# RWKV attention and a leaky-ReLU MLP: w loaded into all partitions and as columns, stage 1 in float32 by hardware queues, dummy matmuls until the first turning

## The chip, the cores and the metric

The kernel runs on one core of a Trainium2 chip. Five engines with instruction streams of their own work side by side and meet at semaphores: TensorE (PE, matmuls), VectorE (DVE), ScalarE (ACT), GpSimd (POOL) and SyncE (SP, here only transfers). The metric is the device time of one execution in microseconds, the median of several runs. A profiled execution shows when each instruction ran; its span goes from the first to the last instruction.

## The reference

Linear attention with a decaying state, over batch 4, 8 heads, 768 positions and head width 48, and behind it an MLP with a leaky ReLU:

```python
state = zeros((B, H, D, D))
for t in range(S):
    kt, vt, rt = k[:, :, t], v[:, :, t], r[:, :, t]
    cur = einsum('bhd,bhe->bhde', u[None] * kt, vt)
    y[:, :, t] = einsum('bhd,bhde->bhe', rt, state + cur)
    state = w[None, :, :, None] * state + einsum('bhd,bhe->bhde', kt, vt)
x = y.transpose(0, 2, 1, 3).reshape(3072, 384)
h = x @ w_in                      # 384 x 2048
out = maximum(0.01 * h, h) @ w_out  # 2048 x 384
```

All inputs and the output are float32; w and u are one vector of 384 numbers each (8 heads times 48).

## The kernel before

**Tiling.** The 4 x 768 positions are cut into 24 stages of 128 (`L`), six to a batch. Inside a stage, the positions lie on the 128 partitions. Powers of w are put into two tables, `qtab` = w^(t-64) and `ktab` = w^(63-t), one row for each position t of the stage, 384 columns. They are the exponentials of t times ln w, so that r * qtab and k * ktab carry the decay between two positions.

**One stage n** goes through named steps:

- P (`prep`): DVE multiplies r by qtab and k by ktab into `qk`, in bf16. r comes first, then k.
- T (`turn`): PE turns the products with the identity (two halves, four matmuls each) into PSUM, and ACT copies both halves into `tp`. From stage 8 on a transfer does this instead.
- A (`a_mm`): eight matmuls of turned k and turned r give the 128 x 128 scores of each head. M (`a_mask`): DVE multiplies them by a triangular mask into `at`.
- X (`diag`): DVE multiplies turned r by turned k into `prod`. K (`kv_mm`): PE multiplies `prod` by the column w*u (`wu`), which gives the share of the current position, and k by v for the state. Q (`prep2`) puts the first into `vs` on DVE. S (`state`): DVE multiplies the new state by the decay table `wl` = w^128.
- Y (`y_part`): PE adds everything up, ACT copies it into `xT`.
- G, J: first matrix product of the MLP (`g1`, `g1_pair`) with the leaky ReLU on ACT; H and `g2_seven`: the second product.

**Order.** Every engine executes its instructions in the order in which `add` was called; semaphore waits come from what is read and written. Up to stage 9 the order is written out by hand in `ORDER`, a list of these letters with the stage's number. Then a loop over pairs of stages goes on. PSUM banks are handed out in rotation by `next_bank`, eight in all.

**Opening.** w and u arrive as one row on one partition each (SP's and ACT's queue). r and k of stage 0 come as float32, r on SP's queue and k on ACT's. All other tiles of r, k and v are cast to bf16 by POOL's queue, one after another, together with the MLP's weights, in the order of `LOADS`. In that list `id` and `tri` stand for the identity and the triangular mask, which POOL makes between its transfers; `wi` and `wo` are the four parts of w_in and of w_out. PE runs `EARLY` = 2 dummy matmuls of 128 x 512 (L255), then spreads the row of w over 128 partitions with two matmuls against a row of ones (L295). ACT takes the logarithm from PSUM in two halves (L298) and makes the tables (L299, L301). The step C (`decay_columns`, L449) turns w and w*u from rows into columns with sixteen matmuls of one column; ACT takes the logarithm of one (`wcol`, L465) and DVE copies the other (`wu`, L467). The step W (`decay_table`, L471) makes `wl` on ACT (L474). U (`u_table`) spreads u over the partitions later on; the cast of u's row to bf16 (L303) stands in the opening.

The lines that the text speaks of are L327 and L329 (P), L379 and L386 (matmuls and copies of T), L399 (A), L417 (M), L334 (X), L429 to L438 (K), L342 (Q), L483 (S), L518 (Y), L546 and L563 (G and J).

Of the kernel before, what the change touches and what calls it, by code (L numbers as in the profile page):

```python
# [17 lines left out]
E = 64  # L18
# [5 lines left out]
FIRST, EARLY = 6, 2  # L24
LOADS = """r1 k1 r2 id k2 wi0 v1 r3 tri k3 v2 wi1 k4 r4 v3 wi2 k5 r5 r6 k6 v4 v5 k7 wi3 r7 v6 v7 wo3 wo2 wo1 wo0"""
ORDER = """
P0 C W P1 T0 A0 X0 M0 T1 P2 K0 A1 T2 Q0 X1 Y0 A2 S0 M1 K1 X2 G0.0 Q1 P3 S1 Y1 T3 K2 M2 G1.0 X3 A3 U J0.2 S2 Q2 M3 Y2 K3 P4 T4 Q3
J0.3 S3 Y3 J0.4 J0.5 J1.0 P5 A4 J1.1 P6 X4 M4 T5 X5 J1.2 K4 Q4 A5 S4 T6 J1.3 K5 J1.4 Y4 M5 L8 Q5 Y5 P7 J1.5 A6 J0.6 J2.0 J2.1 T7
M6 X6 X7 K6 J2.2 J2.3 A7 S6 J2.4 J2.5 L9 Q6 J0.7 J1.6 J2.6 M7 L10 J2.7 L11 J1.7 K7 S7 P8 Q7 Q8 P9 H0 Q9 K8 H1 P10 L12 K9 H2 S8 S9
Y6 Y7 A8 A9 P11 M8 H3 M9 L13  # L30
# [90 lines left out]
def bass_rwkv5_eagle__then__act_leaky_relu_kernel(  # L121
# [13 lines left out]
    def SB(name, shape, dt=BF16):  # L135
        return ctx.enter_context(nc.sbuf_tensor(name, shape, dt))
# [11 lines left out]
    w_row = SB("w_row", [1, HD], FP32)  # L148
    u_row = SB("u_row", [1, HD], FP32)
    one_row = SB("one_row", [1, 128], FP32)  # L150
# [4 lines left out]
    k0_f = SB("k0_f", [128, HD], FP32)  # L155
    r0_f = SB("r0_f", [128, HD], FP32)
# [6 lines left out]
    wu_row = SB("wu_row", [1, HD])  # L163
# [27 lines left out]
    taken = [0]  # L191
# [9 lines left out]
    def load_first(which):  # L201
        src = {"k": k, "r": r}[which][0].rearrange("h t d -> t h d")[0:L, :, :]
        dst = {"k": k0_f, "r": r0_f}[which]
        eng = {"k": "act", "r": "sp"}[which]
        queue = {"k": A, "r": SP}[which]
        add(eng, lambda: queue.dma_start(dst[:, :].rearrange("p (h d) -> p h d", d=D), src),
            W=[(which, 0)], dma=f"{which}0")
# [38 lines left out]
    add("dve", lambda: V.memset(one_row[:, :], 1.0), W=["one_row"])  # L246
# [12 lines left out]

    half_w = [(next_bank(), slice(NH * i, NH * i + NH)) for i in range(2)]  # L260
# [9 lines left out]
    for name in LOADS.split():  # L270
# [15 lines left out]
    add("dve", lambda: V.memset(v_sb[:, :, :].rearrange("p n (h e) -> p (n h) e", e=E)[:, :, D:E], 0.0), W=["v0"])  # L286
    add("dve", lambda: V.tensor_tensor(wu_row[:, :], w_row[:, :], u_row[:, :], ALU.mult),
        R=["w_row", "u_row"], W=["wu_row"])
# [3 lines left out]
    add("dve", lambda: V.memset(wu[:, :, :], 0.0), W=["wu"])  # L292
    fill(EARLY)
    for (ps_w, key_w), cols in half_w:
        add("pe", lambda ps_w=ps_w, cols=cols: PE.matmul(ps_w[:, 0:NH], one_row[:, :], w_row[:, cols], start=True, stop=True),  # L295
            R=["one_row", "w_row"], W=[key_w, "bc"])
    for i, ((ps_w, key_w), cols) in enumerate(half_w):
        add("act", lambda ps_w=ps_w, cols=cols: A.activation(lnw[:, cols], ps_w[:, 0:NH], AF.Ln), R=[key_w], W=[("lnw", i)])  # L298
        add("act", lambda cols=cols: A.activation(qtab[:, cols], lnw[:, cols], AF.Exp, scale=qexp[:, 0:1]),  # L299
            R=[("lnw", i), "qexp"], W=[("qtab", i)])  # L300
    add("act", lambda: A.activation(ktab[:, :], lnw[:, :], AF.Exp, scale=kexp[:, 0:1]),  # L301
        R=[("lnw", 0), ("lnw", 1), "kexp"], W=["ktab"])
    add("act", lambda: A.activation(u_row16[:, :], u_row[:, :], AF.Copy), R=["u_row"], W=["u_row16"])  # L303
# [5 lines left out]
    def k_of(n):  # L309
        return k_sb[:, n % NRK, :] if n else k0_f[:, :]  # L310

    def r_of(n):
        return r_sb[:, n % NRK, :] if n else r0_f[:, :]

    def prep(n):
        iq = n % NQK
        if n >= TURNED:
            both = rk_sb[:, n % NRK, :, :].rearrange("p w (h d) -> p (w h) d", d=D)
            by = tab[:, :, :].rearrange("p w (h d) -> p (w h) d", d=D)
            add("dve", lambda: V.tensor_tensor(qk[iq][:, :, 0:D], both, by, ALU.mult),  # L320
                R=[("r", n % NRK), ("k", n % NRK), ("qtab", 0), ("qtab", 1), "ktab", ("qk0", iq)], W=[("qp", iq), ("kp", iq)])
# [5 lines left out]
        add("dve", lambda: V.tensor_tensor(qk[iq][:, 0:H, 0:D], hd(r_of(n)), hd(qtab[:, :]), ALU.mult),  # L327
            R=[("r", n % NRK), ("qtab", 0), ("qtab", 1), ("qk0", iq)], W=[("qp", iq)])
        add("dve", lambda: V.tensor_tensor(qk[iq][:, H:2 * H, 0:D], hd(k_of(n)), hd(ktab[:, :]), ALU.mult),  # L329
            R=[("k", n % NRK), "ktab", ("qk0", iq)], W=[("kp", iq)])  # L330
# [40 lines left out]
    def turn(n):  # L371
        it, iq = n % NTP, n % NQK
        for half in ((0, 1) if n == 0 else (1, 0)):
# [75 lines left out]
    def decay_columns():  # L449
        ps_c, key_c = next_bank()  # L450

        def emit():
            for hh in range(2):
                for p in range(NP):
                    c0 = (2 * p + hh) * D
                    rows = slice(64 * hh, 64 * hh + D)
                    PE.matmul(ps_c[rows, p:p + 1], w_row[:, c0:c0 + D], one_row[:, 0:1], start=True, stop=True)
                    last = PE.matmul(ps_c[rows, NP + p:NP + p + 1], wu_row[:, c0:c0 + D], one_row16[:, 0:1],
                                     start=True, stop=True)
            return last  # L460

        add("pe", emit, R=["one_row", "one_row16", "w_row", "wu_row"], W=[key_c, "wcols"])
# [269 lines left out]

    def u_table():
# [5 lines left out]
    steps = {"U": u_table, "P": prep, "Q": prep2, "T": turn, "A": a_mm, "M": a_mask, "K": kv_mm, "S": state, "Y": y_part, "X": diag, "C": decay_columns, "W": decay_table, "F": fill,  # L739
# [118 lines left out]
```

## Time and profile before

| | us |
|---|---|
| median of 3 runs | 168.59 (167.9 to 169.27) |
| the profiled execution | 168.52 |
| its span | 166.8 |
| PE busy | 160.0 |
| DVE busy | 120.3 |
| ACT busy | 116.6 |
| POOL busy | 81.8 |

The profiled execution took 168.52 us as timed, of which the span of the trace is 166.8; the rest lies outside the instructions. Busy time is the sum over an engine's instructions; matmuls overlap, so that a busy PE isn't one at its peak. "L255 PE MATMUL a<-b x2" reads: line 255, engine, operation, result and operands, number. A bracket gives the idle time in front of an instruction and what ended it. "Landing" of a transfer is the time at which its semaphore says that all of it is there.

### The profile page before, as it was taken

The numbers are of one execution on the slowest core, as the hardware profiler recorded it, in microseconds if no ns is written. First come the engines' busy times: TensorE is split into PE (matmuls) and PEld (weight loads), VectorE is DVE, ScalarE is ACT, GpSimd is POOL, SyncE is SP. The second block draws the span as 40 slices with busy tenths as digits, with TensorE's granted clock in tenths as the row PEclk, the third lists the DMA queues.
The fourth block names the chain that finished last, engine by engine and source line by source line (L and its number), as shares of the span: only waits on it lengthen the run. The fifth ranks groups of instructions, "written<-read, shape, count | busy, mean of one in ns | idle before, by whom it ended". The sixth has DMA issues, their size and how long they took to land.

```text
span 166.8 us, 5326 instructions
## 1 busy us (share of the span) xinstructions
PE 160.0 (96%) x2264; PEld 132.2 (79%) x2264; DVE 120.3 (72%) x231; ACT 116.6 (70%) x265; POOL 81.8 (49%) x97
## 2 busy tenths in 40 slices
PE   6699999999999999999999999999999999999994
PEld 3578677788666875875876889889899898898993
DVE  7697866653898969999359997986998467046253
ACT  4944877798313771879989889989999845828530
POOL 7999999991179989795660750930000000000000
DMA  5999999999989999999995994995706202002022
GB/s 95 112 146 171 171 149 173 201 192 141 142 201 150 129 92 92 135 162 107 176 178 55 207 119 76 188 114 94 132 4 139 81 4 94 4 4 94 0 98 94
DMA packets 99259, 19.68 MB, mean 118 GB/s; under 512 B 92322, under 2 KB 99236, under 8 KB 99236
## 3 DMA queue, kind: packets, MB, share of 16 engines
q0 software_dynamic: 76512, 10.03, 94.4%
q1 hardware_dynamic: 21682, 9.11, 25.7%
q8 instruction: 18, 0.29, 0.7%
q10 hardware_dynamic: 1042, 0.20, 0.6%
q14 instruction: 5, 0.04, 0.1%
HBM read 20.45 MB, written 4.72 MB: 151 GB/s over the span
## 4 chain that ended last, share of the span: by engine, by line
PE 90%; ACT 5%; DVE 2%; issue 1%; ACTq 0%
PE ps_all L563 36%; PE ps_all L644 20%; PE ps_all L580 16%; PE ps_all L518 7%; PE ps_all L399 5%; ACT tp L386 2%; PE ps_all L433 2%; PE ps_all L379 2%; DVE at L417 1%; PE ps_all L546 1%; PE ps_all L255 1%; PE ps_all L295 1%; ACT tab L299 1%; ACT wl L474 0%; ACT gT L569 0%
## 5 line engine op out<-in xcount | busy, mean ns | idle before, releaser
L563 PE MATMUL ps_all<-xT,w_in_sb 128*128 128x256 bf16 x564 | 64.8, 273 | 0.0
L563 PEld LDWEIGHTS ps_all<-xT,w_in_sb 128*128 128x128 bf16 x564 | 54.3, 98 | 7.2 <-issue 0.2
L569 ACT ACTIVATE gT<-ps_all 128x512 bf16<-128x512 f32 x94 | 55.1, 598 | 6.8 <-PE ps_all L563 2.9
L218 POOL DMA_DIRECT2D rk_sb<-in_k_dram x23 | 21.3, 928 | 16.6 <-PE ps_all L563 16.6
L580 PE MATMUL ps_all<-w_out_sb,gT 128*128 128x384 bf16 x160 | 27.2, 326 | 0.0
L409 DVE CAST_PREDICATED at<-mask,ps_all 128x1024 bf16<-128x1024 uint16 x16 | 18.8, 1219 | 9.2 <-PE ps_all L399 9.2
L367 ACT ACTIVATE at<-ident,s_tok 128x128 bf16<-128x128 bf16 x80 | 24.9, 393 | 0.0
L580 PEld LDWEIGHTS ps_all<-w_out_sb,gT 128*128 128x128 bf16 x160 | 15.3, 98 | 9.7
L218 POOL DMA_DIRECT2D v_sb<-in_v_dram x24 | 22.3, 934 | 0.4 <-issue 0.4
L218 POOL DMA_DIRECT2D rk_sb<-in_r_dram x23 | 21.1, 919 | 0.0
L361 POOL TENSOR_TENSOR at<-ident,s_tok 128x512 bf16<-128x512 bf16 x12 | 13.4, 1140 | 10.4 <-DVE s_tok L351 10.4
L675 DVE TENSOR_TENSOR out_sb<-ps_all,snap 128x192 f32<-128x192 f32 x22 | 7.8, 356 | 14.5 <-PE ps_all L644 13.8
L644 PE MATMUL ps_all<-tw,gs 128*128 128x192 bf16 x168 | 16.0, 246 | 0.0
L586 ACT ACTIVATE out_sb<-ps_all 128x384 f32<-128x384 f32 x10 | 4.9, 488 | 14.5 <-PE ps_all L580 14.4
L644 PEld LDWEIGHTS ps_all<-tw,gs 128*128 128x128 bf16 x168 | 14.0, 98 | 0.0
L533 ACT ACTIVATE xT<-ps_all 128x384 bf16<-128x384 f32 x24 | 11.0, 492 | 4.0 <-PE ps_all L518 3.7
L518 PE MATMUL ps_all<-at,v_sb 128*32 128x128 bf16 x384 | 11.9, 224 | 0.0
L417 DVE TENSOR_TENSOR at<-ps_all,mask 128x512 bf16<-128x512 f32 x16 | 10.3, 683 | 2.2 <-PE ps_all L399 1.9
L618 DVE TENSOR_TENSOR gs<-gT 128x1024 bf16<-128x1024 bf16 x14 | 9.6, 685 | 2.9 <-ACT gT L569 2.9
L644 PE MATMUL ps_all<-w_out_sb,gT 128*128 128x192 bf16 x112 | 11.6, 246 | 0.0
L386 ACT ACTIVATE tp<-ps_all 128x512 bf16<-128x512 f32 x16 | 8.7, 596 | 3.8 <-PE ps_all L379 3.7
L518 PEld LDWEIGHTS ps_all<-at,v_sb 128*32 128x32 bf16 x384 | 9.1, 98 | 2.3 <-issue 1.1
(80 smaller groups left out, 217.5 us busy)
## 6 DMA issues: line engine op xcount, KB each, us to landing
out_dram<-out_sb SPq DMA_DIRECT2D x22, 192.0 KB, 2.4
v_sb<-in_v_dram POOLq DMA_DIRECT2D x24, 96.0 KB, 5.9
rk_sb<-in_r_dram POOLq DMA_DIRECT2D x23, 96.0 KB, 6.0
rk_sb<-in_k_dram POOLq DMA_DIRECT2D x23, 96.0 KB, 5.7
w_in_sb<-in_moe_w_in_dram POOLq DMA_DIRECT2D x4, 384.0 KB, 7.0
w_out_sb<-in_moe_w_out_dram POOLq DMA_DIRECT2D x4, 384.0 KB, 9.7
out_dram<-out_sb SPq DMA_DIRECT2D x4, 96.0 KB, 1.6
tp<-qk SPq DMA_TRANSPOSE x16, 3.4
```

What stands on the lines that cost most here:

```text
L218: add("pool", lambda: G.dma_start(dst, src), R=pace, W=[key], dma=f"{which}{n}")
L361: add("pool", lambda hh=hh, s_of=s_of: G.tensor_tensor(at[ia][:, hh, :, :], ident[:, :].unsqueeze(1).to_broadcast([128, NP, 128]), s_of.un ...
L367: add("act", lambda h=h: A.activation(at[ia][:, h % 2, h // 2, :], ident[:, :], AF.Copy, scale=s_tok[n % 2][:, h:h + 1]), R=["ident", ("s" ...
L386: add("act", lambda dst=dst, ps_t=ps_t: A.activation(dst, ps_t[:, :], AF.Copy), R=[key], W=[("tp", it, half)])
L409: add("dve", lambda: V.copy_predicated(at[n % NAT][:, :, :, :].rearrange("p two m i -> p (two m) i"), mask[:, :].bitcast(mybir.dt.uint16). ...
L417: add("dve", lambda hh=hh, part=part: V.tensor_tensor(at[n % NAT][:, hh, :, :], part, mask[:, :].unsqueeze(1).to_broadcast([128, NP, 128]) ...
L518: last = PE.matmul(ps_y[32 * q:32 * q + 32, 128 * s:128 * s + 128], a, m, start=first_mm, stop=last_mm)
L533: add("act", lambda: A.activation(xT[m % NX][:, :, 128 * half:128 * half + 128], ps_y[:, 0:HD].rearrange("p (s t) -> p s t", t=128), AF.Copy),
L563: last = PE.matmul(ps_g[:, 256 * f:256 * f + 256], w_in_sb[:, s, 128 * fb:128 * fb + 128], xT[ix][:, s, :], start=s == 0, stop=s == NSL - 1)
L569: add("act", lambda: A.activation(gT[ig][:, 2 * j:2 * j + 2, :].rearrange("p f t -> p (f t)"), ps_g[:, :], AF.Prelu, alpha=0.01), R=[key], ...
L580: last = PE.matmul(ps_o[:, 0:HD], gT[ig][:, s, 128 * half:128 * half + 128], w_out_sb[:, s, :], start=s == 0, stop=s == NFB - 1)
L644: done = PE.matmul(ps_o[:, 0:NH], lhs[:, s, :], rhs[:, s, :], start=first and s == 0, stop=s == HF - 1, skip_group_check=not (first and last))
```

## The change

w is loaded by one transfer into all 128 partitions (`w_all`), so the broadcast matmuls and one pair of activations go. w and u are also loaded as columns, two transfers for each (`load_columns`, pieces of 4 bytes), and step C becomes step B, which takes Ln of the one and multiplies the two on DVE. r and k of stage 1 come like those of stage 0, as float32 on SP's and ACT's queue, ahead of the columns; they leave POOL's list. The identity and the mask stand further ahead in that list. u's row comes last on SP's queue, and its cast is a step of its own (V). `EARLY` goes from 2 to 8 dummies, and two single dummies (F1) are put into the order. T1 is cut into its two halves, the half with r in front of A0. `taken` starts at 3, so that later banks are the same as before. DVE's memset of the gaps in v moves behind the other memsets.

```diff
-FIRST, EARLY = 6, 2
-LOADS = """r1 k1 r2 id k2 wi0 v1 r3 tri k3 v2 wi1 k4 r4 v3 wi2 ...
+FIRST, EARLY = 6, 8
+LOADS = """r2 id k2 tri v1 wi0 r3 k3 v2 wi1 k4 r4 v3 wi2 ...
 ORDER = """
-P0 C W P1 T0 A0 X0 M0 T1 P2 K0 A1 T2 Q0 X1 Y0 A2 S0 M1 K1 X2 G0.0 Q1 P3 S1 Y1 T3 K2 M2 G1.0 X3 ...
+P0 T0 P1 B T1.0 F1 A0 T1.1 X0 M0 K0 W P2 F1 A1 V T2 Q0 X1 Y0 S0 M1 K1 A2 X2 G0.0 Q1 P3 S1 Y1 T3 K2 M2 G1.0 X3 ...
...
-    def load_first(which):
-        src = {"k": k, "r": r}[which][0].rearrange("h t d -> t h d")[0:L, :, :]
-        dst = {"k": k0_f, "r": r0_f}[which]
+    def load_first(n, which):
+        src = {"k": k, "r": r}[which][0].rearrange("h t d -> t h d")[n * L:n * L + L, :, :]
+        dst = {"k": k_f, "r": r_f}[which][n]
...
+    def load_columns(h, dst, name):
+        for hh in range(2):
+            add("sp", lambda hh=hh: SP.dma_start(dst[64 * hh:64 * hh + D, :], dram(h, D * hh, [[1, D], [2 * D, NP]]),
+                                                     allow_slow_non_contiguous=True),
+                W=[f"{name}{hh}"], dma=f"{name}{hh}")
...
-    add("sp", lambda: SP.dma_start(w_row[:, :], row(w)), W=["w_row"], dma="w")
-    add("act", lambda: A.dma_start(u_row[:, :], row(u)), W=["u_row"], dma="u")
-    load_first("r")
-    load_first("k")
+    add("sp", lambda: SP.dma_start(w_all[:, :], dram(w, 0, [[0, 128], [1, HD]])), W=["w_all"], dma="w")
+    load_first(0, "r")
+    load_first(0, "k")
+    load_first(1, "r")
+    load_first(1, "k")
+    load_columns(w, w_col, "wc")
+    load_columns(u, u_col, "uc")
+    add("sp", lambda: SP.dma_start(u_row[:, :], row(u)), W=["u_row"], dma="u")
...
-    for i, ((ps_w, key_w), cols) in enumerate(half_w):
-        add("act", lambda ps_w=ps_w, cols=cols: A.activation(lnw[:, cols], ps_w[:, 0:NH], AF.Ln), R=[key_w], W=[("lnw", i)])
-        add("act", lambda cols=cols: A.activation(qtab[:, cols], lnw[:, cols], AF.Exp, scale=qexp[:, 0:1]),
-            R=[("lnw", i), "qexp"], W=[("qtab", i)])
+    add("act", lambda: A.activation(lnw[:, :], w_all[:, :], AF.Ln), R=["w_all"], W=["lnw"])
+    add("act", lambda: A.activation(qtab[:, :], lnw[:, :], AF.Exp, scale=qexp[:, 0:1]), R=["lnw", "qexp"], W=["qtab"])
...
-    def turn(n):
+    def turn(n, *halves):
-        for half in ((0, 1) if n == 0 else (1, 0)):
+        for half in halves or ((0, 1) if n == 0 else (1, 0)):
...
     def decay_columns():
-        ps_c, key_c = next_bank()
...
         for hh in range(2):
             rows = slice(64 * hh, 64 * hh + D)
-            add("act", lambda rows=rows, hh=hh: A.activation(wcol[rows, :], ps_c[rows, 0:NP], AF.Ln),
-                R=[key_c], W=[f"wcol{hh}"])
-            add("dve", lambda rows=rows, hh=hh: V.tensor_copy(
-                wu[rows, :, hh:hh + 1].rearrange("p m o -> p (m o)"), ps_c[rows, NP:2 * NP]),
-                R=[key_c, f"wcol{hh}", "wu"], W=[f"wu{hh}"])
+            add("act", lambda rows=rows: A.activation(wcol[rows, :], w_col[rows, :], AF.Ln),
+                R=[f"wc{hh}"], W=[f"wcol{hh}"])
+            add("dve", lambda rows=rows, hh=hh: V.tensor_tensor(
+                wu[rows, :, hh:hh + 1].rearrange("p m o -> p (m o)"), w_col[rows, :], u_col[rows, :], ALU.mult),
+                R=[f"wc{hh}", f"uc{hh}", "wu"], W=[f"wu{hh}"])
```

The step B stands behind P1 on DVE, and its Ln stands on ACT between the copies of T0 and those of T1; W follows the copies of T1, behind them V. A2 has moved behind K1. From there on ORDER is unchanged.

More of the change, by code (lines that the diff above doesn't have):

```diff
@@ L154, in bass_rwkv5_eagle__then__act_leaky_relu_kernel @@
     u_tab = SB("u_tab", [128, HD])
-    k0_f = SB("k0_f", [128, HD], FP32)
-    r0_f = SB("r0_f", [128, HD], FP32)
+    k_f = [SB(f"k{i}_f", [128, HD], FP32) for i in range(2)]
+    r_f = [SB(f"r{i}_f", [128, HD], FP32) for i in range(2)]
     tab = SB("tab", [128, 2, HD])
@@ L258, in fill @@
         add("pe", emit, R=["ones"], W=[("ps", i), f"fill{n}"])
-    half_w = [(next_bank(), slice(NH * i, NH * i + NH)) for i in range(2)]
     def identity():
@@ L292, in bass_rwkv5_eagle__then__act_leaky_relu_kernel @@
     add("dve", lambda: V.memset(wu[:, :, :], 0.0), W=["wu"])
+    add("dve", lambda: V.memset(v_sb[:, :, :].rearrange("p n (h e) -> p (n h) e", e=E)[:, :, D:E], 0.0), W=["v0"])
     fill(EARLY)
[L294 to L303 removed]
+    add("act", lambda: A.activation(lnw[:, :], w_all[:, :], AF.Ln), R=["w_all"], W=["lnw"])
+    add("act", lambda: A.activation(qtab[:, :], lnw[:, :], AF.Exp, scale=qexp[:, 0:1]), R=["lnw", "qexp"], W=["qtab"])
+    add("act", lambda: A.activation(ktab[:, :], lnw[:, :], AF.Exp, scale=kexp[:, 0:1]), R=["lnw", "kexp"], W=["ktab"])
     at_bank, kv_bank = {}, {}
@@ L309, in k_of @@
     def k_of(n):
-        return k_sb[:, n % NRK, :] if n else k0_f[:, :]
+        return k_sb[:, n % NRK, :] if n > 1 else k_f[n][:, :]
     def r_of(n):
-        return r_sb[:, n % NRK, :] if n else r0_f[:, :]
+        return r_sb[:, n % NRK, :] if n > 1 else r_f[n][:, :]
     def prep(n):
```

42 lines of the change are left out of this document (15 added, 27 removed).

## The prediction
> **What bounds the kernel now.** I read the page first, then the busy time in windows, the chain of waits, and the opening instruction by instruction.
>
> ```profile
> span 166.8 us, 5326 instructions
> PE 160.0 (96%) x2264; PEld 132.2 (79%) x2264; DVE 120.3 (72%) x231; ACT 116.6 (70%) x265; POOL 81.8 (49%) x97
> PE   6699999999999999999999999999999999999994
> ```
> TensorE (PE) is busy for 160.0 of 166.8 us, and its idle time lies almost wholly in the first three slices. The change touches nothing behind the first fifteen microseconds, so only that stage can give or take time. In windows:
>
> ```profile
> 1.40:5.00 3.60, 3.35 (x22) 2.08 (x22) 3.22 (x14) 2.50 (x5) 3.59 (x4) 1.00 1.17 142
> 5.00:8.00 3.00, 1.75 (x23) 1.36 (x21) 2.16 (x6) 2.90 (x9) 3.00 (x6) 1.00 2.18 113
> 8.00:10.60 2.60, 2.01 (x24) 1.60 (x24) 1.92 (x5) 1.36 (x3) 2.60 (x4) 1.00 1.07 128
> 10.60:14.30 3.70, 3.62 (x61) 2.70 (x62) 3.13 (x8) 1.61 (x4) 3.70 (x6) 1.00 2.31 160
> ```
> The first pair of numbers is the window and its length, the next is PE's busy time. Between 5.0 and 10.6 PE idles 1.25 + 0.59 us; afterwards it is full. ACT is the full one between 5 and 8 (2.90 of 3.00). The chain of waits goes through it:
>
> ```profile
> 4.79 0.46 ACT tab L299
> ...
> 6.83 0.36 ACT wl L474
> ...
> 7.21 1.09 ACT tp L386 x2
> ...
> 8.35 0.61 PE ps_all L399 x8
> ...
> 15.73 0.70 PE ps_all L518 x40
> ...
> 17.95 0.43 DVE prod L334
> 18.38 0.47 DVE st L483
> 18.85 0.46 DVE vs L342
> 19.31 1.20 DVE at L417 x2
> 20.51 0.26 DVE qk L327
> 20.77 0.28 DVE qk L329
> ...
> 23.05 2.07 PE ps_all L563 x18
> ```
> Tables of w (tab), then the decay columns and table (wcol, wl), hold ACT until 7.19; only then come the copies of the first turning (tp), and A0 starts on PE at 8.35. Around 18 to 21 us the chain lies on VectorE (DVE). From about 23 us it is solid PE work, so what the stage ahead gains or loses is passed to the end nearly whole.
>
> A second thing binds this stage: the same PE instructions are slow first and fast later.
>
> ```profile
> 1.65 1.04 PE L255 MATMUL ps_all<-ones 128*128 128x512 bf16 x2 [1.65 <-DVE ones L247]
> 10.68 0.61 PE L399 MATMUL ps_all<-tp 48*128 48x128 bf16 x8 [0.32 <-ACT tp L386]
> 11.22 1.04 PE L379 MATMUL ps_all<-ident,qk 128*128 128x128 bf16 x8
> L546 PE MATMUL ps_all<-xT,w_in_sb x12: 227/314/314, 14.3 to 15.5; 128*128 128x128 bf16 x12
> 16.33 0.62 PE L379 MATMUL ps_all<-ident,qk 128*128 128x128 bf16 x8
> ```
> Eight turnings take 1.04 us at 11.22 and 0.62 at 16.33, and within the twelve matmuls of L546 the duration falls from 314 ns to 227 for the last, at 15.5. The windows' column of granted clock stays at 1.00, so it isn't the throttle that the profile lists. PE had run without a break since 10.68, that is 4.8 us, when it became fast.
>
> **The change part by part.** The rows for the opening:
>
> ```profile
> 1.19 0.43 SPq L206 DMA_DIRECT2D r_f<-in_r_dram  x1
> 1.34 0.41 ACTq L206 DMA_DIRECT2D k_f<-in_k_dram  x1
> 1.78 1.28 ACT L242 ACT_TABLE_LOAD   x1 [1.78 <-PEq L843]
> 2.45 0.89 POOL L218 DMA_DIRECT2D rk_sb<-in_r_dram  x1
> 2.61 1.14 PEld L295 LDWEIGHTS ps_all<-w_row,one_row 1*128 1x128 f32 x4 [0.84 <-DMA w_row<-in_w_dram]
> 5.15 0.60 ACT L301 ACTIVATE tab<-lnw,kexp 128x384 bf16<-128x384 f32 x1
> 5.34 0.74 DVE L327 TENSOR_TENSOR qk<-r_f,tab 128x384 bf16<-128x384 f32 x1 [0.45 <-DVE wu L292]
> 6.00 0.55 DVE L329 TENSOR_TENSOR qk<-k_f,tab 128x384 bf16<-128x384 f32 x1
> 6.84 0.36 DVE L327 TENSOR_TENSOR qk<-rk_sb,tab 128x384 bf16<-128x384 bf16 x1
> 7.46 0.36 DVE L329 TENSOR_TENSOR qk<-rk_sb,tab 128x384 bf16<-128x384 bf16 x1 [0.26 <-DMA rk_sb<-in_k_dram]
> 9.11 1.29 DVE L417 TENSOR_TENSOR at<-ps_all,mask 128x512 bf16<-128x512 f32 x2 [0.35 <-POOL mask L267]
> ```
> Transfers, from the list of issues (median to landing in us) and from the packets in the window 3.0 to 4.0:
>
> ```profile
> r_f<-in_r_dram SPq DMA_DIRECT2D x1, 192.0 KB, 3.5
> k_f<-in_k_dram ACTq DMA_DIRECT2D x1, 192.0 KB, 4.0
> q10 hardware_dynamic: 821, 0.16, 77.7%
> q1 hardware_dynamic: 532, 0.10, 49.3%
> ```
> and in the window 4.0 to 4.5, q10 (ACT's queue, k0) alone:
>
> ```profile
> q10 hardware_dynamic: 192, 0.03, 48.2%
> ```
> So r0 landed at 1.19 + 3.5 = 4.7 and k0 at 1.34 + 4.0 = 5.3. Two hardware queues together moved 821 + 532 = 1353 packets in that microsecond: 0.76 us for a float32 tile of 1024 packets of 192 bytes. k0's last 192 packets fell in the next half microsecond, so some 0.8 to 1.0 us passed between its last packet and its landing.
>
> Tables. Gone are the broadcast by two matmuls (L295), one Ln, one Exp and the detour through PSUM. New is w in 128 partitions: 192 KB, priced between nothing and a whole tile's 0.76 us more than the single row, which was there at 2.6. I take 0.6, being few long pieces, plus the sharing with k0: about 3.4. The table load ends at 3.06, so it doesn't bind. Then three activations at ktab's 0.60 at most, qtab ready at 4.6 and ktab at 5.2. r0 now stands behind w on SP's queue and shares with k0 and, soon, k1: w (0.6), k0 and r0 (0.76 each) from about 2.0 make 4.1 to 4.3 for the last packet, and 0.8 to landing: 5.05. P0 starts there instead of 5.34: **0.3 us won**. DVE's memsets ahead of P0, in another order now, were through at 4.89 (P0's q had waited 0.45 at 5.34) and there is one memset and one multiplication less: they stay covered by r0, and would bind only if it came before then.
>
> Turning. P0's q ends at 5.8, its k at 6.3; four turnings each, then two copies of half of 1.09 each, now directly behind ktab: done at 7.55 instead of 8.30, **0.75 us won** in all so far. The eight dummies run 7 steps of 0.42 (1.04 less one duration of about 0.62) and one 0.62, 3.56 us from about 1.45: they end at 5.0, before P0's q, and cost nothing unless P0 came sooner. The sixteen small matmuls of the old columns leave a window in which PE idled anyway: nothing.
>
> Stage 1. r1 and k1 leave POOL's queue (two issues of 0.89 us, so everything behind them is issued 1.8 us sooner) and stand behind r0 and k0 on SP and ACT. From 4.0 three queues share the engines: r1, k1 and POOL's v0 are 3 x 0.76 = 2.3 us, with r0's rest until 6.5; landing at 7.3 to 7.4. In the old run P1's q started at 6.84 without waiting for its tile, and its k waited until 7.46. So r1 is **0.5 us later**, not sooner, and P1 in float32 takes 0.55 to 0.74 for each half, not 0.36. The page "DMA: Bandwidth & Descriptors" of the Trainium skill (section "Issuing engines are not separate DMA queues") speaks against this part too: every queue ends on the same 16 engines, and more of them save issue time alone. The packet rows agree, and the sum is made from them.
>
> The new order puts T1.0 before A0. PE is in order, so A0 waits for P1's q: 7.4 + 0.6 = 8.0, four turnings 0.5, one dummy 0.45, A0 at 8.9 instead of 8.35 and ready at 9.5. M0 starts there instead of at 9.11; its mask, which held M0 for 0.35 us before, now stands further ahead in POOL's queue and is ready. Behind it T1.1 and K0 come no later than before. **0.4 us lost** at M0, which takes the whole gain of the head. This 0.4 goes along DVE through P2, Q0, X1 and S0 to M1, which starts at 12.5.
>
> Columns. Four transfers of 192 pieces of 4 bytes replace 16 matmuls, a copy and ACT's Ln on PSUM. They stand behind r1 on SP's queue. If a piece costs what a packet does, 4 x 192 / 1353 = 0.57 us, doubled by sharing with POOL: last packet near 7.6, landing 8.5. DVE reaches wu at about 8.5, behind it X0, which must be done before M0 at 9.5. Price: nothing; the other end is a rival below. The decay table, two activations of 0.36, stands behind T1's copies now, which end at about 10.5, and S0 asks for it at about 12: covered by 0.8 us. A2 stands behind K1 and so waits for S0, done by 12.5, but M2 asks for it only at 15.6: nothing.
>
> The clock. With T1.0, dummy, A0, T1.1, K0, dummy, A1 and T2 PE now has work without a gap from 8.0. If it takes the same 4.8 us as before, it is fast at 12.8, and no later than 2.6 us ahead of the old 15.4. DVE, back to back from M1 at 12.5, has by the chain's rows M1 1.20, X2 0.43, Q1 0.46 (to 14.6), P3 0.54, S1 0.47 and M2 1.20 and is free at 16.8. Y1 follows Q1 with 0.70 at the fast rate, T3's first half needs about 0.35 and its copies 1.09: 16.8 too. X3 can start at 16.9 to 17.0 instead of 17.95. From there to T4 the steps are the old ones: **0.95 us won**. The transfers allow it: POOL's loads come nearly a microsecond sooner, having lost 1.8 us of issue, while the engines carry 1.2 us of new traffic but start on it sooner. Sum: 168.52 (the profiled execution; 1.7 us of it lies outside the span) less 0.95 is 167.57. The median of the runs is 168.59, the same within 0.1: **167.6**.
>
> **The rivals.**
> A, the eight dummies open the clock already at about 5 us. They are 3.56 us of unbroken work, against 4.8 in the old run, which is only an upper bound of what is needed. The page "TensorE: Matmul & The Clock Gate" of the Trainium skill (Part 1) says that the array starts at half clock and that some 3.4 us of sustained work opens it, by a window that runs freely and so ends anywhere in a kernel. Then A0's 0.61 and the turnings' 1.04 shrink like the 0.62 above, M0 starts at 8.85, and DVE is the bound, back to back: M1 at 11.85, 4.3 us from there to the end of M2, X3 at 16.2 and, 0.43 + 0.47 + 0.46 later, M3 at 17.55 instead of 19.31: 1.75 us, 166.8. For it: the length. Against: PE idles again from 5.0 to 5.8 and from 6.9 to 8.0.
>
> B, PE is fast no sooner, because its work before 11 us is of matmuls on 48 rows and short ones. Then the 0.2 to 0.4 us lost at M0 stays: 168.8. For it: the stretch from 8.35 to 10.36 was full as well and changed nothing.
>
> C, slower: the columns come late. If each of the four tiny transfers costs by itself what k0 spent between its last packet and its landing, about 1.0 us, they end at 7.4 + 4.0 = 11.4. DVE waits there in order, with X0, M0, P2 and everything behind queued, and K0 waits on PE; M0 starts at 12.2 instead of 9.5, 2.7 us on top of the sum: 170.3. From 9.6 on it takes back the whole gain, 1:1. For it: pieces of 4 bytes occur nowhere in the trace. Against: the packets' number is small.
>
> That the change doesn't do what it says, for instance that w in all partitions lands later than 4.5, would be covered by the wait for r1, which ends at 7.4 anyway.
>
> **How the numbers follow.** My forecast 38%, A 22%, B 22%, C 18%. About 1% (1.7 us, below 166.9 or above 170.3) is what can be told from no change. Faster: the lower two thirds of A, whose centre lies at the limit and which gains more if A0 comes sooner, and a little of the forecast's lower side, 0.20. Slower: half of C and the tail of B if r1 is later still, 0.12. The rest, 0.68, lies within. The range runs from 0.7 below A, for a sooner M0, to just short of C's centre: 166.1 to 170.0. It leaves out the upper half of C, B's tail and A's edge. The forecast's own range is 167.0 to 168.3.
>
> **What would show it.** P0's q near 5.05, tp's copies directly behind ktab and done near 7.5; r_f's second transfer landing at 7.3, T1.0 on PE at 8.0 with a wait for DVE's qk; M0 at 9.5; the durations of L379's and L546's successors falling from 314 to about 220 ns between 11 and 13 us (at 5 in A, at 15 in B); no wait for a column's transfer before wu (over 0.8 us in C); X3 near 17.0. I am wrong if r1 lands before 6.8, if wu waits, or if solid PE work starts more than a microsecond away from where the sum puts it.

## The result and the profile after

The changed kernel took 173.18 us (median of 4 runs, 172.66 to 174.24), the kernel before 168.69 on the same chip: a ratio of 1.0277, 95% interval 1.0211 to 1.0343. It is slower by 2.8%; 167.6 had been forecast, with a range up to 170.0. Where a ratio stands beside a median below, the ratio leaves out executions more than 1.5% above the fastest one of their kernel.

The profiled execution took 173.44 us, its span 171.7. The page's span, PE's busy tenths and the granted clock in 40 slices of 4.3 us:

```profile
span 171.7 us, 5285 instructions
...
PE   6179999969999999999999999999999999999993
...
PEclk9955899999999999999999999999999999999999
```

PE is all but empty in the second slice, has a new hole in the ninth, and this page has a row of granted clock, which the page of before lacks. The opening instruction by instruction (start, duration, engine, line, operation; in the bracket the idle time ahead and what ended it):

```profile
1.52 3.48 PE L264 MATMUL ps_all<-ones 128*128 128x512 bf16 x8 [1.52 <-DVE ones L256]
...
5.32 0.52 ACT L299 ACTIVATE lnw<-w_all 128x384 f32<-128x384 f32 x1 [2.10 <-DMA w_all<-in_w_dram]
...
7.84 0.56 DVE L325 TENSOR_TENSOR qk<-r_f,tab 128x384 bf16<-128x384 f32 x1 [3.51 <-DMA r_f<-in_r_dram]
...
8.55 1.01 PE L377 MATMUL ps_all<-ident,qk 128*128 128x128 bf16 x8 [3.54 <-DVE qk L325]
...
10.03 0.56 DVE L325 TENSOR_TENSOR qk<-r_f,tab 128x384 bf16<-128x384 f32 x1 [1.16 <-DMA r_f<-in_r_dram]
...
12.00 0.16 DVE L452 TENSOR_TENSOR wu<-w_col,u_col 48x4 bf16<-48x4 f32 x1 [0.29 <-DMA u_col<-in_u_dram]
...
12.54 1.28 DVE L415 TENSOR_TENSOR at<-ps_all,mask 128x512 bf16<-128x512 f32 x2
```

The steps ahead of M0 (12.54, before 9.11) end waits for transfers: w's tile at 5.3, r0 at 7.8, r1 at 10.0, the last column of u at 12.0. Between the dummies' end at 5.0 and T0 at 8.55 PE has nothing to do. The chain of waits (start, length, what):

```profile
2.34 3.59 SPq L211
6.97 5.00 DMA u_col<-in_u_dram
12.54 1.28 DVE at L415 x2
...
24.21 0.62 PE ps_all L377 x8
...
34.77 0.65 PE ps_all L548 x5
35.42 1.57 issue
37.60 2.07 PE ps_all L548 x18
```

It starts with the issue of one column transfer, which alone held SP's queue for 3.59 us. T4 (the row at 24.21) stood at 21.10 before: 3.11 of the 4.9 us of span are lost by then. The next 1.57 are "issue": PE stops in the middle of a group of six matmuls and waits for no semaphore.

### The profile page after: what moved, and what is told of

Its sections match the earlier page's. It is cut to its first block, busy times and chain, and to the rows that moved or that the text cites. A ratio compares the mean times of both kernels' runs of the same rounds, so it can differ in the third digit from the quotient of the medians.

```text
span 171.7 us, 5285 instructions
## 1 busy us (share of the span) xinstructions
PE 160.3 (93%) x2244; PEld 130.2 (76%) x2244; DVE 119.6 (70%) x229; ACT 116.4 (68%) x263; POOL 80.0 (47%) x95
## 2 busy tenths in 40 slices
DMA packets 100233, 20.08 MB, mean 117 GB/s; under 512 B 93169, under 2 KB 100210, under 8 KB 100210
## 3 DMA queue, kind: packets, MB, share of 16 engines
q0 software_dynamic: 74432, 9.84, 86.9%
## 4 chain that ended last, share of the span: by engine, by line
PE 85%; SPq 3%; DVE 3%; DMA 3%; ACT 2%; issue 1%
PE ps_all L548 36%; PE ps_all L629 19%; PE ps_all L565 15%; PE ps_all L503 7%; PE ps_all L397 4%; DMA u_col<-in_u_dram 3%; SPq L211 3%; PE ps_all L431 2%; PE ps_all L377 2%; DVE at L415 1%; ACT tp L384 1%; PE ps_all L531 1%; SPq L206 1%; ACT gT L554 0%; DVE qk L327 0%
## 5 line engine op out<-in xcount | busy, mean ns | idle before, releaser
L224 POOL DMA_DIRECT2D rk_sb<-in_k_dram x22 | 20.1, 912 | 19.3 <-PE ps_all L548 16.4
L224 POOL DMA_DIRECT2D rk_sb<-in_r_dram x22 | 19.9, 904 | 0.0
L377 PE MATMUL ps_all<-ident,qk 128*128 128x128 bf16 x64 | 6.3, 253 | 5.2 <-DVE qk L325 4.6
## 6 DMA issues: line engine op xcount, KB each, us to landing
w_in_sb<-in_moe_w_in_dram POOLq DMA_DIRECT2D x4, 384.0 KB, 10.1
```

What stands on the lines that cost most here:

```text
L224: add("pool", lambda: G.dma_start(dst, src), R=pace, W=[key], dma=f"{which}{n}")
```

## The experiments

Where no number of executions is given, a run has one. The kernel before took 169.17 us beside runs 1 to 4 (one execution), 168.58 (median) beside runs 5 to 8, 168.37 beside 9 to 12, 168.49 beside run 13. The changed kernel's four executions lie up to 1.6 us apart, so a single time is read together with the trace. M0 and T4 are the starts of their first instruction in the profiled execution.

**First group: four parts of the changed kernel, one at a time.**

1. The stop at 35 us: PE's program made longer.

```diff
     fill(EARLY)
+    tiny(20)
```

`tiny(n)` runs n matmuls of 128 x 128 by one column on the dummies' data.

> The changed kernel with twenty more dummy matmuls of one column behind the eight, where PE idles from 5.0 to 8.5 us anyway; nothing else differs. In the changed kernel's trace PE stood still for 1.57 us at 35.4, between the fifth and the sixth matmul of one group of L548, which no semaphore separates. Theory F: PE had run out of instructions; it gets them in blocks by a transfer of 16 KB, and the change, with some twenty matmuls fewer in the opening, moved the end of a block into the dense small matmuls of two Y steps. Then the twenty put the blocks back where they were: no stall there, about 171.8 us. Rival: the stall comes from the data, the late parts of w_in, or from the engine itself: it stays, 173.4 us.

Measured: 170.71 us, no wait for "issue" on PE, M0 at 12.49, T4 at 23.56. The stop (1.57) and a T4 that comes 0.65 sooner are 2.2 of the 2.7 us. Theory F's time was 171.8. With the longer program the stop is gone, but run 8 below shows that its place in the program alone does not make it.

2. The columns by sixteen matmuls from w_all's first row, instead of the four transfers.

```diff
-    load_columns(w, w_col, "wc")
-    load_columns(u, u_col, "uc")
...
+                    PE.matmul(ps_c[rows, p:p + 1], w_all[0:1, c0:c0 + D], one_row[:, 0:1], start=True, stop=True)
```

> The changed kernel with the old way to the columns alone: sixteen small matmuls from row 0 of w_all and from w times u, a copy by DVE, and no column transfers; u's row comes behind w_all. Theory C (the columns are what is late, my rival C): M0 started at 12.54 behind wu and X0 at 12.0 and 12.2; without them it starts with A0's end, and if the columns also held up something else, sooner than 11.5: 1 us or more. Theory R (r1 is as late as the columns, because all float32 transfers are late): A0 ended at 12.2 because r1 landed at 10.0, so M0 moves by 0.3 only, and by a little more if r1 no longer shares. With the stall theory F, the added matmuls take that stall away too, another 1.6 us: about 171.5 by R, 170.5 by C.

Measured: 171.63 us; w's tile at 5.0, P0 at 8.38, P1 at 10.48, and M0 at 13.18, later still: r1 comes 0.45 later, now behind u's row too, and the sixteen matmuls in front of T1.0 end 0.4 after P1's q. No stop. The columns' transfers aren't what makes r0 and r1 late, and the time is theory R's.

3. r and k of stage 1 back on POOL's queue in bf16.

```diff
-LOADS = """r2 id k2 tri v1 ...
+LOADS = """r1 k1 r2 id k2 tri v1 ...
...
-    load_first(1, "r")
-    load_first(1, "k")
```

> The changed kernel with r1 and k1 back on POOL's queue in bf16, ahead of r2, as before; all else as changed. Theory Q (too much stands in front of the columns and of r1): the columns land about 2 us sooner, near 10, r1 at 7.5 to 8, M0 starts near 10.5, the head gains 2 us: 171.4 with the stall, 169.8 without. Theory W (w in all partitions is the slow one, and delays r0 and all behind it): r0 still lands at 7.5 or later, M0 gains less than 1 us.

Measured: 171.31 us; w's tile at 4.9, P0 at 7.15, P1 at 9.17, M0 at 11.28, T4 at 22.48, and the stop is there, 1.5 us. Neither theory holds as it stands: r0 lands at 7.1, sooner than W's 7.5, and M0 gains 1.3, between W's 1 and Q's 2. Fewer bytes on the hardware queues help, but w and r0 stay late.

4. w as a row, spread by two matmuls after two of the dummies.

```diff
-    add("sp", lambda: SP.dma_start(w_all[:, :], dram(w, 0, [[0, 128], [1, HD]])), W=["w_all"], dma="w")
+    add("sp", lambda: SP.dma_start(w_row[:, :], row(w)), W=["w_row"], dma="w")
```

> The changed kernel with w as one row and the two broadcast matmuls again (behind two of the eight dummies), the columns still by transfers and r1, k1 still in float32 by hardware queues. Theory W: w's 192 KB from one row of 1.5 KB took until 5.3 to land and pushed r0 from 4.7 to 7.8; without it r0 lands near 5, P0 starts there, r1 lands near 8, M0 starts at 10.5 or sooner: 171.3 with the stall. Theory Q: r0 gains no more than w's share of the bytes, 0.6 to 0.8 us, M0 as much: 172.7.

Measured: 172.78 us. The transfers did as theory W has it: P0 at 5.44 and P1 at 7.47, 2.4 and 2.6 sooner. But DVE waited for the last column until 9.84, and M0 was at 10.38. PE lost its rate meanwhile, here in A0 and A1, the same eight matmuls:

```profile
8.63 0.40 PE L406 MATMUL ps_all<-tp 48*128 48x128 bf16 x8
...
11.15 0.60 PE L406 MATMUL ps_all<-tp 48*128 48x128 bf16 x8
```

From 1.52 to 7.4 it had worked without a gap; between the two rows it waited 1.16 for the columns. T4 came at 22.75, and the stop took 2.0, so that the time missed theory W's 171.3.

**Second group: the parts on the kernel before, and w's transfer by itself.**

5. w into 128 partitions, nothing else.

```diff
-    add("sp", lambda: SP.dma_start(w_row[:, :], row(w)), W=["w_row"], dma="w")
+    add("sp", lambda: SP.dma_start(w_all[:, :], dram(w, 0, [[0, 128], [1, HD]])), W=["w_row"], dma="w")
```

> The kernel before with one part of the change: w by one transfer into 128 partitions, first on SP's queue, and Ln and Exp in one piece from it; columns still by sixteen matmuls, from w's first partition; stage 1 and order as before. Theory W (this transfer by itself costs what was lost): w lands at 4.9 to 5.3 as in the changed kernel, r0 behind it at 6.5, P0 at 7 to 7.8 instead of 5.34, M0 at 10.8 to 11.3 instead of 9.11, T4 at 22.8 to 23.2 instead of 21.10, the time 170.2 to 171.2, and a wait of PE for instructions may come on top. Rival (w is late only in company with the other new transfers): w lands near 3.4, r0 at 5.0, M0 at 9.0 to 9.2, 168.3 to 168.8.

Measured: 169.48 us (median of 10), ratio 1.0055 (1.0037 to 1.0073). w's tile landed at 4.7, near theory W's 4.9 to 5.3, so it is slow by itself; r0 at 6.3, where the changed kernel, with more transfers behind w, has 7.8. P0 started at 6.40, M0 at 9.99, T4 at 22.10. Alone it costs 0.9 us, half of what was expected at M0.

6. Stage 1 in float32 by hardware queues, nothing else.

```diff
+    load_first(1, "r")
+    load_first(1, "k")
...
-LOADS = """r1 k1 r2 id ...
+LOADS = """r2 id ...
```

> The kernel before with one other part: r and k of stage 1 in float32, by SP's and ACT's queue, behind stage 0; w as a row, columns by matmul, order as before. As the prediction counted it: r1 lands at 7.3 to 7.4, P1's q starts there instead of at 6.84, T1 stands behind A0 so that M0 stays at 9.1 and T1's copies wait for nothing new: 168.3 to 168.9. Rival (the two tiles on the hardware queues hold up v0 and r2, which come by POOL): K0 or P2 waits for a transfer and T4 is 0.5 or more later, 169.2 to 170.5.

Measured: 168.47 us (median of 10), ratio 1.0000 (0.9980 to 1.0021); P1 at 6.99, M0 at 9.14. It costs nothing.

7. The order and the dummies, nothing else: 2 + 2 dummies, ORDER and LOADS of the change, columns by matmuls in the opening.

```diff
-P0 C W P1 T0 A0 X0 M0 T1 P2 K0 A1 T2 ...
+P0 T0 P1 B T1.0 F1 A0 T1.1 X0 M0 K0 W P2 F1 A1 V T2 ...
```

> The kernel before with the order and the dummies of the change alone: w as a row and spread by matmuls, columns by sixteen matmuls in the opening, two more dummies behind these and the two single ones, r1 and k1 by POOL, the decay table behind T1's copies, the mask earlier. Theory (the order is sound, the transfers spoilt it): T0's copies start at 6.7 to 7.0 instead of 7.21, A0 at 8.0 to 8.2, M0 at 8.5 to 8.8 instead of 9.11, the clock opens 1 to 3 us sooner, T4 at 19.3 to 20.5 instead of 21.10, 166.7 to 168.0. Rival (the order itself costs, T1.0 ahead of A0 and the dummies): M0 at 9.1 or later and the same clock, 168.6 to 169.6.

Measured: 167.97 us (median of 10), ratio 0.9957 (0.9937 to 0.9976), between the two: M0 at 9.23 as in the rival, T4 at 20.91 later than the theory's 20.5, the time at the end of the theory's range. The order is no loss.

8. The same transfer in the changed kernel, from 128 different rows.

```diff
-    add("sp", lambda: SP.dma_start(w_all[:, :], dram(w, 0, [[0, 128], [1, HD]])), W=["w_all"], dma="w")
+    add("sp", lambda: SP.dma_start(w_all[:, :], dram(r, 0, [[HD, 128], [1, HD]])), W=["w_all"], dma="w")
```

> The changed kernel, but the transfer into w's tile reads 128 different rows of 1.5 KB (the beginning of r) instead of one row 128 times, and the logarithm is that of a constant 0.95, so the tables don't hold w; same bytes, same pieces, same queue. Theory S (128 pieces that read the same 1.5 KB are served slowly): the transfer lands at 3.4 to 3.9 instead of 5.3, r0 at 5.1 to 5.6 instead of 6.5. Rival (it is the writing of 128 long pieces, or the start of the queue): it lands at 4.9 to 5.3 as before, and r0 at 6.5.

Measured: 168.55 us (one execution), 4.6 less than the changed kernel, by the address of one source. The DMA issues (queue, number, size, us from issue to landing), of the changed kernel and of this one:

```profile
w_all<-in_w_dram SPq DMA_DIRECT2D x1, 192.0 KB, 4.5
```
```profile
w_all<-in_r_dram SPq DMA_DIRECT2D x1, 192.0 KB, 2.8
```

Both were issued at 0.80, so the tile was there at 3.6 instead of 5.3. What follows on its opening:

```profile
3.68 0.61 ACT L301 ACTIVATE lnw<-w_all,wbias 128x384 f32<-128x384 f32 x1 [0.47 <-DMA w_all<-in_r_dram]
...
5.75 0.56 DVE L327 TENSOR_TENSOR qk<-r_f,tab 128x384 bf16<-128x384 f32 x1 [1.38 <-DMA r_f<-in_r_dram]
...
7.85 0.56 DVE L327 TENSOR_TENSOR qk<-r_f,tab 128x384 bf16<-128x384 f32 x1 [1.07 <-DMA r_f<-in_r_dram]
...
10.08 0.16 DVE L454 TENSOR_TENSOR wu<-w_col,u_col 48x4 bf16<-48x4 f32 x1 [0.29 <-DMA u_col<-in_u_dram]
...
10.61 1.28 DVE L417 TENSOR_TENSOR at<-ps_all,mask 128x512 bf16<-128x512 f32 x2
```

(r0's 6.5 in the expectation counts from its issue at 1.26; here it is 4.5.) r0 and r1 come 2.1 and 2.2 sooner than in the changed kernel, M0 1.93 sooner, T4 at 21.40. Theory S holds: the source makes the transfer slow, not its bytes or pieces. The other traces agree: 128 reads of w's row took 3.9 to 4.5 us from issue to landing in six kernels (the changed one, runs 1, 2, 3, 5 and 12), 128 rows of r 2.8 in two (runs 8 and 11). That it is the repeated address, and not w's place in DRAM, is inferred: w's row read once was there at 2.6 in the kernel before, but no run reads 128 different addresses at that place. And the stop on PE is gone, with PE's program unchanged.

**Third group: the rest of the change put together, the columns alone, and the stop.**

9. Runs 6 and 7 together (the line taken out is run 7's), with the decay columns and table on ACT ahead of T0's copies and one dummy behind the columns' matmuls.

```diff
-P0 T0 P1 B T1.0 F1 A0 T1.1 X0 M0 K0 W P2 F1 A1 V T2 ...
+P0 B W T0 P1 T1.0 F1 A0 T1.1 X0 M0 K0 P2 F1 A1 V T2 ...
```

> The order of the change and its float32 stage 1 by hardware queues, without its transfers of w and of the columns: w as a row and spread by matmuls, columns by sixteen matmuls in the opening, one dummy behind them, and the decay columns and table on ACT ahead of T0's copies. Theory (the rest of the change is sound; in the run with the order alone the chain went over POOL's transfers to v, which come 1.8 sooner here): X0 does not wait, M0 at 8.6 to 8.9 instead of 9.11, no wait for v's transfer near 20, T4 at 19.8 to 20.6, 166.8 to 167.7, below the run with the order alone (167.97). Rival (DVE and the clock set the stage, not the transfers): M0 0.3 sooner and T4 no sooner than 20.9, 167.9 to 168.4.

Measured: 167.56 us (median of 12), ratio 0.9959 (0.9936 to 0.9982); M0 at 9.37 missed the theory's 8.6 to 8.9, T4 at 20.08 is in its range. From the opening, M0, two groups of Y0's matmuls and X3:

```profile
9.37 1.29 DVE L436 TENSOR_TENSOR at<-ps_all,mask 128x512 bf16<-128x512 f32 x2 [0.66 <-PE ps_all L418]
...
12.40 0.41 PE L524 MATMUL ps_all<-at,v_sb 128*32 128x128 bf16 x4
...
12.72 0.29 PE L524 MATMUL ps_all<-at,v_sb 128*32 128x128 bf16 x4
...
16.93 0.43 DVE L353 TENSOR_TENSOR prod<-tp 128x512 bf16<-128x512 bf16 x1 [0.29 <-ACT tp L405]
```

Groups of four like matmuls fall from 0.41 to 0.29 between 12.4 and 12.7: PE becomes fast some 3.4 us after M0.

10. The columns by transfer, nothing else, behind r0 on SP's queue.

```diff
     load_first("r")
+    load_columns(w, w_col, "wc")
+    load_columns(u, u_col, "uc")
```

> The kernel before with the columns alone: w and u as columns by the four transfers of 192 pieces, behind r0 on SP's queue; w's row, its spreading, stage 1 and the order as before. Theory (the columns' price is the queue ahead of them): with no long w and no r1 ahead, the issue on SP takes 2 to 4, the last column lands at 6.5 to 7.5, where DVE's products and ACT's table in front of P1 and T0's copies wait for them, M0 at 9.1 to 10.0, 168.6 to 169.6. Rival (the pieces are slow by themselves, as rival C of the prediction had it): they land at 8 to 9 here too, M0 at 10.5 to 11.5, 170 to 171.

Measured: 169.78 us (median of 10, from 168.07 to 170.95), ratio 1.0053 (1.0016 to 1.0090). The theory holds for the landing: DVE has the last column by 6.9, and M0 starts at 9.38. SP's issue of w's two column transfers, of the changed kernel, then of this run:

```profile
2.34 4.10 SPq L211 DMA_DIRECT2D w_col<-in_w_dram  x2
```
```profile
1.67 1.05 SPq L212 DMA_DIRECT2D w_col<-in_w_dram  x2
```

In runs 4 and 8, where r0 and r1 stand ahead without the slow w, it was 2.19 and 2.35 for the two; in run 3, with the slow w and r0 but no r1 ahead, 1.25. So the issue itself takes longer the more is queued ahead, and a slow w alone does not hold it. The time is just above the theory's range. In the profiled execution, at 170.74 one of the long ones, little of it is lost at M0 (0.27), but T4 is at 22.11, 1.01 later than before: T3's turnings at 17.23 take 0.81, those of the kernel before at 16.33 0.62, so PE, without the sixteen matmuls here, is fast later. It also has a stop of PE of 1.25 us at 33.65.

11. Lateness alone: run 8 with a memset on DVE repeated three times ahead of P0.

```diff
-    add("dve", lambda: V.memset(v_sb...
+    for i in range(4):
+        add("dve", lambda: V.memset(v_sb...
```

> The run in which w's transfer reads 128 different rows (tables without w), with the last memset of DVE ahead of P0 repeated three times, 4 us of DVE; PE's program and all transfers are the same as there. It shows what lateness alone does: M0 at 11.3 to 12.0 instead of 10.61, T4 about 1 later, 169.4 to 170.2. Theory L (PE waits for its instructions when its program runs late against the loads of w_out and the next stages): PE stands 1.4 to 2.0 on top of that near 34 us, 171 to 172. Rival (the place of the blocks of instructions in PE's program alone): no such wait, since there was none with the same program.

Measured: 172.04 us, M0 at 12.63, T4 at 23.25, that is 1.85 later than in run 8, and PE's waits (engine, result and line, what for: us in total, times, longest):

```profile
PE ps_all L551 <- issue: 1.5, 1, 1.5
```

1.85 + 1.5 is 3.35 of the 3.5 us between runs 8 and 11. M0 is later than the expected 11.3 to 12.0. Theory L holds in this execution: the same program, late, meets the stop.

12. The changed kernel with the loads of w_out behind the loads of stage 9.

```diff
-... k7 wi3 r7 v6 v7 wo3 wo2 wo1 wo0"""
+... k7 wi3 r7 v6 v7"""
...
-K6 J2.2 J2.3 A7 S6 J2.4 J2.5 L9 Q6 ...
+K6 J2.2 J2.3 A7 S6 J2.4 J2.5 L9 O Q6 ...
```

O issues the four loads.

> The changed kernel with the four loads of w_out issued behind the loads of stage 9 on POOL's queue instead of at 22.7. Theory D (the fetch of PE's next instructions waits behind the long pieces of w_out): no wait of PE for instructions near 35 us, 171.3 to 172.0. Rival (the fetch has its place and time whatever else moves): the wait of 1.5 stays, 173 to 174.

Measured: 172.71 us, T4 at 24.31 (24.21 in the changed kernel), and no wait for "issue". Instead PE waits for w_out:

```profile
PE ps_all L565 <- DMA w_out_sb<-in_moe_w_out_dram: 1.0, 1, 1.0
```

Both traces have packets of 16 KB on an instruction queue (q8), taken here for PE's, since it is PE that stands still behind a late one. One starts at 25.8 to 25.9 in both kernels. The next one starts at 29.8 here, at 34.7 in the changed kernel, where PE stopped at 35.42. The DMA packets of the changed kernel from 31 to 35, then of this run from 30 to 34:

```profile
DMA packets 1255, 0.81 MB, mean 204 GB/s; under 512 B 241, under 2 KB 1254, under 8 KB 1254
```
```profile
DMA packets 4387, 0.42 MB, mean 104 GB/s; under 512 B 4387, under 2 KB 4387, under 8 KB 4387
```

In the changed kernel 1014 of 1255 pieces have 512 bytes or more: that is w_out on its way. Theory D holds for the stop, which is exchanged for 1.0 of waiting, and the time lies above its 171.3 to 172.0.

13. Run 9 with A0 ahead of T1.0.

```diff
-P0 B W T0 P1 T1.0 F1 A0 T1.1 X0 M0 K0 P2 F1 A1 V T2 ...
+P0 B W T0 P1 F2 A0 X0 M0 T1 K0 P2 F1 A1 V T2 ...
```

> As the run with the order and stage 1 together, but with A0 ahead of T1 again, both halves of T1 behind M0's step and two dummies in place of T1.0 and one dummy. Theory M (what M0 loses by waiting for r1 is passed on to T4): A0 at 8.0 to 8.1, M0 at 8.6 to 8.8 instead of 9.37, T4 at 19.3 to 19.7 instead of 20.08, 166.8 to 167.2. Rival (the clock, not M0, sets the stage: with another gap it opens no sooner than 12.8): M0 0.7 sooner and T4 at 20.0 or later, 167.4 to 168.2.

Measured: 166.69 us (median of 6, 166.59 to 166.84), ratio 0.9896 (0.9872 to 0.9920). From the opening:

```profile
8.06 0.61 PE L418 MATMUL ps_all<-tp 48*128 48x128 bf16 x8
...
8.84 1.29 DVE L436 TENSOR_TENSOR at<-ps_all,mask 128x512 bf16<-128x512 f32 x2
...
10.42 0.40 PE L418 MATMUL ps_all<-tp 48*128 48x128 bf16 x8 [0.35 <-ACT tp L405]
...
11.85 1.28 DVE L436 TENSOR_TENSOR at<-ps_all,mask 128x512 bf16<-128x512 f32 x2
```

M0 is 0.53 sooner than in run 9, PE is fast already in A1 at 10.42 (0.61 at 8.06, 0.40 here), and T4 starts at 19.42. Theory M holds, with M0 0.04 later and the time 0.1 shorter than its ranges. But two things changed together, M0 and the time at which PE is fast; the second is taken up below. This version beats both kernels, the one before by 1.0%.

## Why the prediction was wrong

The forecast's span was 165.85 (166.8 less 0.95); 171.7 came. M0 was 3.04 later than the sum's 9.5; from M0 to T4 it took 11.67 where the sum had 10.65 (20.15 less 9.5), 1.02 more; the stop took 1.57. That is 5.63 of 5.85; 0.2 stays unassigned. The 3.04 come from the transfers, the 1.02 from the clock.

**Tables: the step that failed.** "New is w in 128 partitions: 192 KB, priced between nothing and a whole tile's 0.76 us more than the single row ... I take 0.6", there at 3.4. By run 8 that price fits 192 KB from 128 different rows (3.6). One row read 128 times came at 5.3, 1.7 later, and everything behind it on SP's queue was late: r0 at 7.8 instead of 5.05, and P0 and T0 with it. Run 8, with the other address alone, wins back 1.93 at M0 and 2.81 at T4. The 5.05 itself was short as well: r0 came at 5.7 in run 8 and at 5.4 in run 4, where w is one row. The upper end of the bounds was a tile read from different addresses, which is not the same operation; nothing in the trace of before bounded it. So the term of the sum that failed is w's 0.6, with the sharing 0.8: from the single row's 2.6 to 5.3 it was 2.7.

**The cover that wasn't one.** A late w, the prediction said, "would be covered by the wait for r1, which ends at 7.4 anyway". r1 stands behind w on the same queue: it landed at 10.0. In run 8 it came at 7.85, without the long w in run 6 by 7.0, in run 4 by 7.5. The estimate for stage 1 was good; the cover moved with what it should cover.

**Stage 1 and T1.0 before A0.** A0 at 8.9 and M0 at 9.5 were forecast; run 9, without the transfers of w and the columns, has 8.64 and 9.37. The price of the place, 0.4, is shown by run 13: 0.53 at M0. At T4 it is 0.66, of which 0.13 falls behind M0, where PE is fast sooner.

**Columns, "Price: nothing".** Landing at 8.5 was forecast, 12.0 came in the changed kernel, 10.1 in run 8, before 7 alone. The pieces by themselves were no slower than forecast (run 10); their issue and landing stretch with the queue ahead. In run 8, A0's eight matmuls (9.43, 0.61 long) end at 10.04 and M0 starts at 10.61 behind wu and X0; in run 9 it follows A0's end by 0.12, so the columns hold it by some 0.45. Rival C's 170.3 with M0 at 12.2 came near at M0 for another reason: run 2 has no column transfer and M0 at 13.18.

**The clock.** "Fast at 12.8" and "X3 at 16.9 to 17.0" were forecast with M0 at 9.5. Run 9 shows 12.7 and 16.93, and its 167.56 is the forecast's 167.6. But run 9 is not the kernel of the sum (w is a row, the columns come by matmul, ACT's order differs), so that the total agrees is in part luck; what it bears out is the piece from M0 on. In the changed kernel PE was fast only at 18.4, 5.9 us after M0, X3 at 21.06. Its windows (PE's busy time after the length, the granted clock third from the end):

```profile
5.00:8.00 3.00, 0.00 (x1) 0.00 (x0) 0.16 (x1) 1.64 (x3) 3.00 (x4) 1.00 1.54 178
8.00:12.00 4.00, 2.37 (x21) 1.51 (x21) 2.05 (x5) 2.09 (x5) 4.00 (x6) 0.52 2.08 133
...
16.00:20.00 4.00, 4.00 (x93) 3.01 (x86) 3.90 (x9) 1.67 (x5) 4.00 (x5) 0.70 1.99 172
```

PE is empty from 5.0 to 8, and then the granted clock stands at 0.52. So the slow rate is that of the granted clock, and the prediction was wrong that "it isn't the throttle that the profile lists": the column shows 1.00 until the trace has a first change, and in the trace of before none was recorded. A mean of 0.52 over 8 to 12 puts the fall at about 8.2, if the clock goes from 1 to 0.5, and one of 0.70 over 16 to 20 the return at 18.4. The single records of the granted clock, which the trace keeps beside its instructions, say the same and more: full from 4.76, half from 8.17, full from 18.41. In all traces that have such records, the stretches between two changes last 3.41 us or a multiple of it (here 3.41 and 10.24).

The idle time before the fall is 3.2 us. The page "TensorE: Matmul & The Clock Gate" of the Trainium skill (Part 1) has the gate close after an idle window of about 3.4 us, and the changed kernel is near that; in run 4 it closed although the longest wait was 1.16, and PE was busy for 1.82 of the 3.41 us for which the clock was full.

The clock is where the 1.02 behind M0 comes from. In the table, full clock is the start of the record that shows it, counted from M0:

| kernel | M0 to full clock | M0 to T4 |
|---|---|---|
| run 11 | 3.28 | 10.62 |
| run 9 | 3.48 | 10.71 |
| run 3 | 4.81 | 11.20 |
| changed | 5.87 | 11.67 |
| run 7 | 5.88 | 11.68 |
| run 4 | 7.46 | 12.37 |

The later PE is fast, the longer X3 waits for the copies of T3: 0.20 in run 11, 1.10 in the changed kernel, 1.81 in run 4. The sum had 3.3 (12.8 less 9.5) and 10.65, so its step from M0 to T4 was right for the clock that it assumed. What it could not forecast is when the clock opens. The "same 4.8 us" of unbroken work is no rule: the kernel before and run 6 have the same program on PE and M0 at 9.11 and 9.14, and PE is fast at about 15.4 in one and at 16.3 in the other.

Rival A had the eight dummies open the clock at about 5. That happened in the changed kernel's profiled execution, at 4.76, but PE had nothing to do from 5.0 to 8.55, and by then the clock had fallen again. In run 3 T0 came in time: the clock was full from 5.85 to 9.26, T0's eight turnings at 7.85 took 0.77 with a pause for k among them, and T1.0's four at 9.59 took 0.61. It does not happen each time. The mean granted clock of the changed kernel's four executions is 0.97, 0.99, 1.00 and 0.97, and in run 8, 1.3 us behind the same dummies, T0's eight turnings took 1.01, the slow rate, and the first record of a full clock is at 14.29. Run 13 met rival A's numbers by another way. M0 at 8.85, M1 at 11.85, X3 at 16.2 and 166.8 us were its numbers, and 8.84, 11.85, 16.27 and 166.69 came. But A had M0 sooner by fast turnings and a fast A0, and run 13's A0 took 0.61, the slow rate; M0 is sooner there because A0 does not wait for r1. That DVE is then the bound, almost back to back from M0 to M3, is as A had it; that the numbers of M0 agree is luck.

**The stop: not in the prediction.** "From there to T4 the steps are the old ones", and from T4 on "solid PE work" had been taken for granted. PE's next block of instructions, 16 KB, came late (run 12). In the five kernels whose trace has a stop (the changed one, runs 3, 4, 10 and 11) the third such packet starts 8.6 to 9.0 us behind the second, in all others 4.0 to 6.2. A late opening can let the fetch fall among the loads of w_out (run 11), but lateness does not decide it: run 10 stops with T4 at 22.11, run 5 does not with T4 at 22.10, nor run 2 at 24.41. The page "DMA: Bandwidth & Descriptors" of the Trainium skill (section "Queues, rings and completion order") says that a DMA engine takes its queue rows in turn, a packet of descriptors at a time. The runs agree in so far as the fetch comes sooner when w_out's pieces are away; that it waits its turn on one engine is not shown. What decides stays open; the fetches of runs 1 and 2, whose programs are longer by 20 and 16 matmuls, were in time at much the same lateness as the changed kernel's.

## What to carry to other kernels

A broadcast read of one row of DRAM into all partitions is not a tile's load: price it as its own operation, and put nothing urgent behind it on its queue. Where a wait is said to cover a delay, check that what it waits for doesn't stand behind the same delay. When the same instructions run at two rates in the opening, find in each trace when they become fast before a gain or a loss is put down to anything else, and look for the cost of lateness as far as the next fetch of instructions.

## What the runs showed of the hardware

- 128 reads of 1.5 KB from one address landed 3.9 to 4.5 us after the issue (six kernels), from 128 addresses after 2.8 (two).
- Transfers of pieces of 4 bytes hold the issuing queue by what stands ahead of them: 1.05 us for two behind r0, 1.25 behind the slow w and r0, 2.19 to 2.35 behind r0 and r1, 4.10 behind the slow w, r0 and r1.
- Instructions come in packets of 16 KB over the DMA engines. With one late, PE stopped for 1.25 to 2.0 us, with no semaphore in the wait.
- A clock once open closes again within the opening: in run 4, PE was fast at 8.6 and slow at 11.15, with no wait over 1.16 between them and a busy time of 1.82 of 3.41 us. The column of granted clock is silent on the slow start and shows only what follows the first recorded change; in four traces (before, runs 5, 10 and 13) it records none, although the same instructions turn fast.
